# Gated linear attention and a squared-ReLU layer on one core: wider tiles for y of the first eight blocks, and another written-out order

## The chip, the cores and the metric

The kernel runs on one core of a Trainium2 chip. The metric is the device time of one execution in microseconds (us). Three runs of the kernel before gave 184.23, 184.34 and 184.44 us; the median is 184.34 us. Names of engines: PE multiplies matrices (PEld are its weight loads), DVE is VectorE, ACT is ScalarE, POOL is GpSimd, SP issues the DMAs.

## What is computed

The reference has two parts. The first is a recurrence over 768 time steps for 4 batches and 8 heads of 48 channels:

```
state = alpha[t, :, None] * state + outer(k[t], v[t])
y[t]  = q[t] @ state
```

The second takes y of all heads as rows of 384 numbers (3,072 rows) and computes

```
h = x @ w_in                        # 384 -> 2048
g = s * max(h, 0)**2 + b
out = g @ w_out                     # 2048 -> 384
```

All inputs and the output are in float32; the kernel multiplies in bfloat16.

## The kernel before

**Blocks.** The 3,072 rows are cut into 24 blocks of 128 rows, numbered n; six blocks make one batch. Blocks 0 to 7 are worked on as four pairs m = 0 to 3 (functions with a 2 in their name), with even and odd time steps in two halves s and with the two blocks c of the pair in rows 0 to 63 and 64 to 127. Blocks 8 to 23 are worked on one by one (functions with a 1).

**The attention of a block.** `ln2` (ACT) takes logarithms of alpha; `cum2` and `blk2`, or `cumA` (PE), sum them along time; `eb` and `ei` (ACT) turn the sums into factors; `mul` (DVE or POOL) scales q and k with them. For pairs 0 to 2, `T2` transposes q and k on PE and `Tc2` copies the result out of PSUM; pair 3 and the single blocks are transposed by a DMA (`T1`, line 616). `A2` or `A1` (PE, lines 496 and 638) multiply k by q, `mk` (DVE) masks the result into `am`. `KV2` or `KV1` (PE, lines 481 and 625) make the sum over k and v, and `t1` (DVE) and `sn` (POOL or DVE) carry the state on.

**y.** `y2(m)` (line 544) makes y of a pair, and `y1(n)` (line 660) that of a single block. The values v lie in `vp`, which has for each pair p of heads a row of VW = 144 columns: 48 values of one head, 48 zeros, 48 values of the other. y2 makes its output in tiles of 32 channels: a product takes 32 columns of `vp` as weights (64 rows, one block c) and 128 columns of `am`. Sixteen entries of the list `OWN` say which head (p, e) adds to which tile x; with two halves s and two blocks c these are 64 products of 64 rows by 32 columns in each pair. Where a tile of 32 reaches past a head's 48 channels, the zeros of `vp` are in the product. Twelve products with the state follow for each block that has one (line 556, 128 rows by 32 columns). Outputs go to the PSUM banks py (c = 0) and ct (c = 1). `ye` copies y from there to `xd`.

**The second part.** Two blocks make a group g (12 groups). `mm1(g,u,w)` (line 732, six products) makes one of eight units u of h into the bank h_ps[w]; `re` (ACT line 742 or DVE line 744) takes the maximum with zero and `sq` (DVE or POOL line 761, ACT line 759) squares it into `gt`. `mm2(n,jq)` (line 766, four products) adds a quarter of w_out's rows to block n's output in o_ps[n % 2]; `oe` (DVE, line 775) scales and adds the bias, `st` stores. The last block is made in two halves (`mm2h`, `oeh`, `sth`).

**Weights.** `ld_i` and `ld_o` load w_in and w_out in four parts each into staging tiles; `cih` and `co` cast them to bfloat16 (lines 333 and 335); `cp`, `ca` and `cf` (line 359) sum w_out's rows for the bias, and `bmm` and `bc` (lines 379 and 384) spread that sum over o_ps[1] and into `bias_w`.

**Order.** The string PROGRAM holds the whole order, written out by hand: each word calls a function, with its arguments and often the engine behind dots (`re.0.3.0.0.ACT`: group 0, unit 3, bank 0, buffer 0, on ACT). Every engine and SP's DMA queue takes its own words strictly in that order and waits at the first whose inputs are not there. `F.n.w.bank` are fillers: n products of zeros, w columns wide, into a bank that is free. `c_...` words set constants, among them `c_vp` (POOL, line 268), which writes the zeros of `vp`. Below, a word such as mm1.0.6 stands for group 0, unit 6; bank and buffer are left out where they do not matter.

Of the kernel before, what the change touches and what calls it, by code (L numbers as in the profile page):

```python
# [37 lines left out]
mul2.q.1.0.DVE A2.0.0.a c_s.0 mk2.0.1.0 ld_o.1 mul2.k.1.0.POOL mk2.0.1.1 F.2.480.c T2.1.0.o0 mk2.0.0
KV2.0 mul2.k.1.1.POOL Tc2.1.0.o0.ACT ld2.a.2 t1.0 c_t1.1 vc2.1.1.ACT F.2.296.c T2.1.1.o1 vc2.1.0.ACT
y2.0 Tc2.1.1.o1.DVE ld2.v.2 t1.1 A2.1.1.o ye.1.ACT A2.1.0.a ye.0.ACT sn.1.POOL mk2.1.0 cih.1.1.ACT KV2.1  # L40
c_V2 cih.1.0.ACT mm1.0.3.0 t1.2 ld2.q.2 mm1.0.2.1 mk2.1.1.0 sn.2.POOL re.0.3.0.0.ACT mk2.1.1.1
cih.0.0.ACT cih.0.1.POOL t1.3 sq.0.3.0.ACT ld2.k.2 c_ones sn.3.DVE re.0.2.1.1.ACT F.5.456.a0 y2.1
cp.1.DVE ld_o.0 mm1.0.1.0 ye.2.ACT ye.3.DVE ln2.2 mm1.0.0.1 co.1.DVE ld_i.3 sq.0.2.1.ACT cum2.2.1
re.0.1.0.2.DVE cum2.2.0 re.0.0.1.0.ACT blk2.2 ld_i.2 vc2.2.1.DVE eb2.2.1 mm1.1.2.0 sq.0.1.2.DVE ei2.2.0
mm1.1.3.1 sq.0.0.0.DVE ei2.2.1 ld_o.3 mul2.q.2.1.DVE re.1.2.0.1.ACT el2.2 eb2.2.0 mm1.1.0.0
mul2.k.2.1.DVE sq.1.2.1.ACT mul2.k.2.0.DVE re.1.3.1.2.ACT mul2.q.2.0.DVE T2.2.1.y ld2.a.3 vc2.2.0.DVE
T2.2.0.c Tc2.2.1.y.ACT mm1.1.1.1 co.0.POOL Tc2.2.0.c.DVE sq.1.3.2.ACT KV2.2 re.1.1.1.0.DVE A2.2.0.a
re.1.0.0.1.ACT ld_o.2 cp.0.POOL mk2.2.0 mm2.0.0 sq.1.1.0.ACT cih.3.0.ACT mm2.0.1 t1.4 A2.2.1.a
cih.3.1.ACT mm1.0.6.1 sq.1.0.1.DVE ld2.v.3 sn.4.POOL mk2.2.1 mm1.0.7.0 ld_bs re.0.6.1.2.ACT cih.2.1.DVE
mm1.1.7.1 re.0.7.0.0.ACT cih.2.0.DVE sq.0.7.0.ACT mm1.1.6.0 ld2.k.3 ca.0.1.DVE re.1.7.1.1.ACT y2.2  # L50
sq.1.7.1.ACT sq.0.6.2.DVE ld2.q.3 cp.3.DVE re.1.6.0.0.ACT mm1.1.5.1 ye.4.ACT sq.1.6.0.POOL ye.5.DVE
mm1.0.4.0 ln2.3 re.1.5.1.2.DVE re.0.4.0.1.ACT cum2.3.1 co.3.DVE ld1.v.9 mm1.2.3.1 sq.0.4.1.ACT
sq.1.5.2.ACT mm1.0.5.0 co.2.POOL re.2.3.1.0.DVE ld2.a.4 eb2.3.1 cum2.3.0 re.0.5.0.1.DVE ei2.3.1 blk2.3
bsm mm1.2.0.1 sq.2.3.0.ACT bsc vc2.3.0.POOL ld2.a.6 ei2.3.0 mm1.2.5.0 sq.0.5.1.DVE re.2.0.1.2.ACT
cp.2.DVE mm2.0.2 vc2.3.1.ACT ld1.k.9 re.2.5.0.0.ACT mul2.k.3.0.DVE mm1.2.6.1 sq.2.0.2.ACT mul2.k.3.1.DVE
mm1.1.4.0 mul2.q.3.1.DVE eb2.3.0 mm2.0.3 re.2.6.1.1.ACT ca.2.3.DVE T1.7 sq.2.5.0.ACT mm1.2.1.1
mul2.q.3.0.DVE el2.3 re.1.4.0.2.ACT KV2.3 ca.0.2.DVE T1.6 sq.1.4.2.ACT mm1.2.4.0 sq.2.6.1.ACT cf.DVE
re.2.1.1.0.DVE bmm ld1.q.11 ld1.q.10 sq.2.1.0.POOL mm1.2.7.1 bc ld1.k.10 oe.0 mm2.1.0 ld1.k.11
re.2.4.0.2.DVE mm2.1.1 t1.6 sq.2.4.2.ACT mm2.1.2 ln2.4 mm2.2.0 A2.3.0.a mm2.1.3 mk2.3.0 ld1.k.8 mm2.2.1
re.2.7.1.1.DVE mm2.2.2 ld1.v.10 t1.7 A2.3.1.a mm2.2.3 ld1.q.8 mk2.3.1 mm1.2.2.0 ld1.q.9 oe.1 y2.3 blk2.4  # L60
ld1.v.8 ye.6.DVE ye.7.ACT mm2.3.0 re.2.2.0.0.ACT oe.2 cumA.4 ld2.a.5 sq.2.2.0.POOL mm2.3.1 st.0 ei1.9
ei1.8 mm1.3.5.1 mul1.k.9.DVE ld1.v.12 sq.2.7.1.ACT mul1.k.8.DVE mm1.3.7.0 el2.4 re.3.5.1.2.ACT ld1.q.13
sn.7.POOL mm2.3.2 eb1.8 re.3.7.0.0.ACT mul1.q.8.DVE mm1.3.4.1 ln2.6 sq.3.5.2.DVE T1.8 mm2.4.0
re.3.4.1.1.DVE vc1.8.POOL eb1.9 mm2.3.3 vc1.9.POOL st.1 mul1.q.9.DVE KV1.8 mm1.3.6.0 t1.8 T1.9 mm1.3.1.1
re.3.6.0.2.ACT sq.3.4.1.DVE sn.8.POOL KV1.9 ln2.5 mm2.4.1 oe.3 st.2 c_U sq.3.7.0.ACT t1.9 mm1.3.0.0
ld2.a.7 re.3.1.1.1.ACT sq.3.6.2.DVE blk2.5 mm2.5.0 ld1.q.12 sn.9.POOL ld1.q.14 cumA.5 sq.3.1.1.DVE A1.8
vc1.10.POOL eb1.10 mm1.3.3.1 mk1.8 ei1.10 mm2.5.1 ei1.11 re.3.0.0.0.ACT mul1.k.10.DVE mm2.5.2 eb1.11
mul1.q.10.DVE re.3.3.1.2.ACT mm2.5.3 sq.3.0.0.DVE T1.10 sq.3.3.2.ACT mul1.k.11.DVE mm1.3.2.0
mul1.q.11.DVE KV1.10 oe.5 mm2.4.2 re.3.2.0.1.ACT T1.11 t1.10 el2.5 mm2.4.3 ln2.7 sq.3.2.1.POOL A1.9 oe.4
ld1.k.13 mm2.7.0 sn.10.POOL mk1.9 st.4 mm2.6.0 ld1.k.12 mm2.7.1 st.3 Ayy.10 ld2.a.11 ld1.v.13 mm2.6.1  # L70
ye.8.DVE ye.9.ACT vc1.12.POOL mk1.10 mm2.7.2 ld2.a.8 mm1.4.1.1 blk2.6 mm1.4.2.0 re.4.1.1.0.ACT
sq.4.1.0.DVE cumA.6 ld1.v.11 re.4.2.0.2.ACT A1.11 mm1.4.4.1 ei1.12 sq.4.2.2.DVE eb1.12 mul1.k.12.DVE
mm2.7.3 el2.6 re.4.4.1.1.ACT mul1.q.12.DVE mm2.6.2 eb1.13 mk1.11 T1.12 mm1.4.3.0 sq.4.4.1.DVE mm1.4.0.1
re.4.3.0.0.ACT mul1.q.13.DVE ld1.q.15 mm2.6.3 vc1.13.POOL ld1.v.14 re.4.0.1.2.ACT sq.4.3.0.DVE mm1.4.6.0
ei1.13 sq.4.0.2.DVE oe.6 KV1.12 mm1.4.7.1 re.4.6.0.1.ACT mul1.k.13.DVE mm2.8.0 vc1.11.POOL t1.12 T1.13
mm1.4.5.0 sq.4.6.1.DVE oe.7 Ayy.12 re.4.5.0.0.ACT ld1.q.16 ld1.k.14 ld2.a.9 mm2.8.1 ye.10.DVE ye.11.ACT
st.5 re.4.7.1.2.ACT sq.4.5.0.DVE blk2.7 mm1.5.4.0 mk1.12 ld1.k.15 KV1.13 mm1.5.5.1 re.5.4.0.1.ACT
sq.4.7.2.DVE mm2.9.0 t1.13 re.5.5.1.0.ACT mm1.5.6.0 sq.5.4.1.DVE sn.13.POOL ld1.v.15 A1.13
re.5.6.0.2.ACT cumA.7 vc1.14.POOL mk1.13 mm1.5.3.1 ld1.v.16 eb1.14 ei1.14 mm1.5.1.0 re.5.3.1.1.ACT
sq.5.6.2.DVE mul1.q.14.DVE mm2.8.2 el2.7 re.5.1.0.2.ACT mul1.k.14.DVE mm2.8.3 eb1.15 sq.5.3.1.DVE T1.14  # L80
ei1.15 sq.5.1.2.DVE mm1.5.2.1 sq.5.5.0.DVE mm2.9.1 re.5.2.1.1.ACT st.6 mul1.k.15.DVE mm1.5.0.0 oe.8
mm2.9.2 re.5.0.0.2.ACT vc1.15.POOL st.8 mm1.5.7.1 st.7 sq.5.0.2.DVE sq.5.2.1.DVE KV1.14 ld1.q.17
mm2.10.0 re.5.7.1.0.ACT t1.14 ln2.8 mm2.10.1 mul1.q.15.DVE mm2.10.2 sq.5.7.0.DVE T1.15 sn.14.POOL Ayy.14
ld1.k.16 mm2.10.3 ye.13.ACT mk1.14 vc1.16.POOL ld1.k.17 ye.12.ACT ld1.q.22 mm2.9.3 ld1.v.22 oe.10
mm1.6.1.0 blk2.8 KV1.15 re.6.1.0.2.ACT mm1.6.4.1 sq.6.1.2.DVE mm1.6.3.0 t1.15 re.6.4.1.1.ACT A1.15 oe.9
sn.15.POOL cumA.8 ld2.a.10 mm1.6.0.1 eb1.16 ei1.16 mul1.q.16.DVE mm2.11.0 re.6.0.1.0.ACT mul1.k.16.DVE
mm2.11.1 eb1.17 sq.6.4.1.DVE T1.16 ei1.17 sq.6.0.0.DVE mm2.11.2 re.6.3.0.2.ACT mul1.k.17.DVE mm2.11.3
el2.8 mk1.15 st.9 mm1.6.2.1 ld1.k.18 ld1.v.17 oe.11 mm1.6.6.0 re.6.2.1.1.ACT KV1.16 mm2.13.0
sq.6.2.1.DVE re.6.6.0.0.ACT t1.16 mm1.6.5.1 mul1.q.17.DVE mm1.6.7.0 sq.6.3.2.DVE T1.17 sn.16.POOL Ayy.16
re.6.7.0.1.ACT ln2.9 ld1.q.18 mm2.12.0 ye.14.ACT ye.15.DVE ld1.q.19 re.6.5.1.2.ACT sq.6.7.1.DVE ld1.k.19  # L90
mm2.13.1 ln2.10 ld1.v.18 sq.6.5.2.DVE mm1.7.0.0 sq.6.6.0.DVE st.10 mk1.16 mm1.7.4.1 vc1.17.POOL
re.7.0.0.1.ACT mm2.13.2 re.7.4.1.2.ACT blk2.9 sq.7.4.2.DVE mm1.7.6.0 ld1.q.23 A1.17 re.7.6.0.0.ACT
cumA.9 mk1.17 mm2.12.1 ei1.19 ld1.v.19 eb1.19 mm1.7.1.1 el2.9 sq.7.0.1.DVE eb1.18 mm2.13.3 ei1.18
mul1.q.18.DVE re.7.1.1.2.ACT mm1.7.7.0 mul1.k.18.DVE sq.7.1.2.DVE T1.18 mm1.7.2.1 mul1.q.19.DVE
re.7.7.0.1.ACT mul1.k.19.DVE mm2.12.2 re.7.2.1.2.ACT sq.7.7.1.DVE mm1.7.3.0 ld1.q.20 ln2.11 oe.13
vc1.18.POOL ld1.k.20 mm2.12.3 sq.7.2.2.DVE re.7.3.0.1.ACT T1.19 mm2.15.0 oe.12 KV1.18 vc1.19.POOL
mm1.7.5.1 ld1.q.21 sq.7.3.1.DVE mm2.14.0 t1.18 st.13 re.7.5.1.2.ACT ld1.v.20 mm2.14.1 st.12 Ayy.18 st.11
ld1.k.21 mm2.15.1 ye.16.ACT ye.17.DVE sq.7.6.0.DVE KV1.19 mm1.8.5.0 sq.7.5.2.DVE mk1.18 mm1.8.6.1
re.8.5.0.1.ACT blk2.10 mm1.8.7.0 re.8.6.1.0.ACT t1.19 A1.19 sq.8.6.0.DVE re.8.7.0.2.ACT cumA.10
sq.8.5.1.DVE mm1.8.3.1 sn.19.POOL mk1.19 el2.10 ei1.20 eb1.20 mm2.14.2 re.8.3.1.0.ACT mul1.k.20.DVE  # L100
# [761 lines left out]
```

## Time and profile before

| | |
|---|---|
| median of three runs | 184.34 us (184.23 to 184.44) |
| the profiled execution, its own time | 184.03 us |
| its span, first to last instruction | 182.3 us |
| PE busy | 171.9 us, 2,309 products |
| DVE busy | 136.6 us |
| ACT busy | 103.8 us |
| POOL busy | 47.2 us |
| products of zeros (fillers) | 21 |
| moved by DMA | 34.96 MB |

The profile counts an engine as busy from the start of an instruction to its modelled end; products overlap, so distances from start to start say more about PE than busy time. A view called the chain of waits follows the work back from the last instruction; the timeline lists instructions by start; a table by stretches gives each engine's busy time in a stretch of the span. Times inside the execution are counted from its first instruction.

### The profile page before, as it was taken

The numbers are of one execution on the slowest core, as the hardware profiler recorded it, in microseconds if no ns is written. First come the engines' busy times: TensorE is split into PE (matmuls) and PEld (weight loads), VectorE is DVE, ScalarE is ACT, GpSimd is POOL, SyncE is SP. The second block draws the span as 40 slices with busy tenths as digits, with TensorE's granted clock in tenths as the row PEclk, the third lists the DMA queues.
The fourth block names the chain that finished last, engine by engine and source line by source line (L and its number), as shares of the span: only waits on it lengthen the run. The fifth ranks groups of instructions, "written<-read, shape, count | busy, mean of one in ns | idle before, by whom it ended". The sixth has DMA issues, their size and how long they took to land.

```text
span 182.3 us, 5580 instructions
## 1 busy us (share of the span) xinstructions
PE 171.9 (94%) x2309; PEld 122.5 (67%) x2309; DVE 136.6 (75%) x257; ACT 103.8 (57%) x204; POOL 47.2 (26%) x79
## 2 busy tenths in 40 slices
...
GB/s 156 325 355 375 276 338 374 365 271 212 196 217 211 156 158 260 163 234 155 214 238 202 190 223 153 151 214 185 250 58 154 79 96 150 2 5 86 0 133 86
DMA packets 101357, 34.96 MB, mean 192 GB/s; under 512 B 94548, under 2 KB 99796, under 8 KB 101332
## 3 DMA queue, kind: packets, MB, share of 16 engines
...
q8 instruction: 18, 0.29, 0.6%
q14 instruction: 7, 0.06, 0.1%
...
## 4 chain that ended last, share of the span: by engine, by line
PE 75%; DVE 10%; DMA 6%; SPq 3%; issue 3%; POOL 1%; ACT 1%; DVEq 0%; POOLq 0%
PE o_ps L766 31%; PE h_ps L732 28%; SPq L294 3%; DMA qkT<-qk 3%; PE a_ps L638 3%; DMA k_in<-in_k_dram 3%; DVE colsum L359 3%; DVE am L509 2%; PE py_ps L660 2%; PE ct_ps L660 2%; PE ct_ps L571 2%; PE py_ps L625 1%; POOL qk L447 1%; DVE t L701 1%; DVE r L744 1%
## 5 line engine op out<-in xcount | busy, mean ns | idle before, releaser
L732 PE MATMUL h_ps<-xd,w_in_bf 128*128 128x256 bf16 x576 | 74.2, 273 | 0.8 <-DVE r L744 0.6
L742 ACT ACTIVATE r<-h_ps 128x512 bf16<-128x512 f32 x87 | 51.8, 599 | 40.7 <-PE h_ps L732 36.8
L766 PE MATMUL o_ps<-w_out_bf,gt 128*128 128x384 bf16 x368 | 69.3, 326 | 0.1
L732 PEld LDWEIGHTS <-w_in_bf 128*128 128x128 bf16 x576 | 54.6, 98 | 13.7 <-issue 2.9
L766 PEld LDWEIGHTS <-gt 128*128 128x128 bf16 x368 | 34.3, 98 | 19.4 <-issue 0.9
L761 DVE TENSOR_TENSOR gt<-r 128x512 bf16<-128x512 bf16 x74 | 34.3, 484 | 13.4 <-ACT r L742 12.8
L711 POOL TENSOR_TENSOR s_st<-t,blast 128x384 bf16<-128x384 bf16 x15 | 14.6, 971 | 38.8 <-DVE t L701 35.8
L647 DVE TENSOR_TENSOR am<-a_ps,U 128x1024 bf16<-128x1024 f32 x16 | 19.5, 1219 | 3.8 <-PE a_ps L638 3.7
L335 POOL CAST vp<-v_in 128x384 bf16<-128x384 f32 x18 | 11.6, 646 | 33.4 <-DMA v_in<-in_v_dram 24.4
L775 DVE SCALAR_TENSOR_TENSOR o_sb<-o_ps,bs,bias_w 128x384 f32<-128x384 f32 x23 | 14.1, 613 | 3.8 <-PE o_ps L766 2.2
L759 ACT ACTIVATE gt<-r 128x512 bf16<-128x512 bf16 x18 | 11.1, 628 | 3.8 <-DVE r L744 3.7
L333 ACT ACTIVATE xd<-ct_ps 128x384 bf16<-128x384 f32 x6 | 2.9, 490 | 15.2 <-PE ct_ps L660 8.6
L394 ACT ACTIVATE la<-a_in 128x768 bf16<-128x768 f32 x12 | 10.1, 841 | 2.4 <-DMA a_in<-in_alpha_dram 2.4
L761 POOL TENSOR_TENSOR gt<-r 128x512 bf16<-128x512 bf16 x4 | 4.7, 1164 | 23.3 <-ACT r L742 12.3
L595 DVE TENSOR_TENSOR qk<-k_in,binv 128x384 bf16<-128x384 f32 x16 | 9.7, 612 | 1.2 <-ACT binv L585 1.1
L509 DVE TENSOR_TENSOR am<-a_ps,mask 128x1024 bf16<-128x1024 f32 x6 | 7.3, 1223 | 3.9 <-PE a_ps L496 3.7
L595 DVE TENSOR_TENSOR qk<-q_in,b_s 128x384 bf16<-128x384 f32 x16 | 9.7, 606 | 0.6 <-ACT b_s L581 0.4
L701 DVE TENSOR_TENSOR t<-py_ps,s_st 64x192 bf16<-64x192 f32 x26 | 9.2, 353 | 0.9 <-PE py_ps L625 0.5
L335 DVE CAST xd<-ct_ps 128x384 bf16<-128x384 f32 x6 | 3.3, 556 | 5.1 <-PE ct_ps L660 5.0
L447 DVE TENSOR_TENSOR qk<-q_in,b_s 128x384 bf16<-128x384 f32 x7 | 3.8, 556 | 4.3 <-ACT b_s L424 4.3
L824 PE MATMUL a_ps<-zeros 128*128 128x504 bf16 (+3 forms) x17 | 5.7, 478 | 1.3 <-DVE zeros L215 1.3
L333 ACT ACTIVATE xd<-py_ps 128x384 bf16<-128x384 f32 x8 | 3.9, 487 | 5.0 <-PE py_ps L660 3.6
...
## 6 DMA issues: line engine op xcount, KB each, us to landing
...
```

The lines of the kernel that those rows point to most:

```text
L335: {"DVE": nc.vector, "POOL": nc.gpsimd}[eng].tensor_copy(out=out, in_=in_)
L509: nc.vector.tensor_tensor(out=o, in0=i, in1=mask2[s].rearrange("a t p -> a (t p)").unsqueeze(1).to_broadcast([128, n, 128]), op=ALU.mult,)
L595: on(eng).tensor_tensor(out=half_of(qk, n)[:, "qk".index(x), :, 0:D], in0=half_of(ins[x], n).rearrange("a (h d) -> a h d", d=D), in1=half_ ...
L647: nc.vector.tensor_tensor(out=half_of(am, n).rearrange("a e p t -> a (e p) t"), in0=a_ps.rearrange("a e (p t) -> a (e p) t", t=128), in1=U ...
L701: nc.vector.tensor_tensor(out=t1_sb[n % 2][r, :, w], in0=p_ps[r, :, w], in1=s_sb[(n - 1) % 4][r, :, w], op=ALU.add,)
L711: on(eng).tensor_tensor(out=s_sb[n % 4], in0=t1_sb[n % 2], in1=bl.unsqueeze(2).to_broadcast([128, NP, 96]), op=ALU.mult,)
L732: nc.tensor.matmul(out=h_ps[w][:, i * n : (i + 1) * n], lhsT=w_in_bf[:, kk, 128 * j : 128 * (j + 1)], rhs=xd_sb[g % 3][:, kk, 0:n], start= ...
L742: nc.scalar.activation(out=r_sb[i], in_=h_ps[w], func=AF.Relu)
L759: nc.scalar.activation(out=unit_out(g, u), in_=r, func=AF.Square)
L761: on(eng).tensor_tensor(out=unit_out(g, u), in0=r, in1=r, op=ALU.mult)
L766: nc.tensor.matmul(out=o_ps[n % 2][:, 0:d_model], lhsT=gt_of(n)[:, j, c0 : c0 + C], rhs=w_out_bf[:, j, :], start=(j == 0), stop=(j == NJ - 1),
L775: nc.vector.scalar_tensor_tensor(out=out_sb[n % 3], in0=o_ps[n % 2][:, 0:d_model], scalar=s_col, in1=bias_w, op0=ALU.mult, op1=ALU.add,)
```

## The change

The layout `vp` gets 48 more columns of zeros for each pair of heads (VW = 192), so that a window of 64 columns can run past a head at either side. y2 makes y of all four pairs in tiles of 64 channels: twelve entries in `OWN64`, two tiles at a time, which with the two blocks makes four products in a row for four different quarters of the array; with s there are 48 products of 64 by 64 in each pair instead of 64 of 64 by 32. The products with the state and those of the single blocks keep their 32 columns. The order of the words is another one from the first to the last, and some words have another engine: re on DVE 7 instead of 9 (ACT 89 instead of 87), ye on DVE 11 instead of 10, vc2 (the copy of v) on ACT 7, DVE 0, POOL 1 instead of 4, 2, 2, mul2 on POOL 4 instead of 3, cih on POOL 2 instead of 1. The sq keep their numbers (74 on DVE, 18 on ACT, 4 on POOL), though not their places. The fillers are 18 products instead of 21.

```diff
-VW = 144
+
+VW = 192
+Y64 = (0, 1, 2, 3)
...
-c_zeros ld2.a.0 c_act c_qk.1 c_half c_vp.1 ld2.a.1 c_qk.0 ld2.q.0 c_la.1 ld2.k.0 c_la.0 c_s.2 c_t1.0
...
+c_zeros ld2.a.0 c_act c_la.0 c_half c_s.0 ld2.a.1 c_la.1 ld2.q.0 c_qk.0 c_qk.1 ld2.k.0 c_U2 c_ident
+ln2.0 ld2.q.1 c_vp.1 c_t1.0 F.8.504.a0 cum2.0.0 c_vp.0 ld2.k.1 ln2.1 blk2.0 c_mask2 cum2.0.1 eb2.0.0
+cum2.1.0 ld2.v.0 mul2.q.0.0.DVE eb2.0.1 cum2.1.1 ei2.0.0 blk2.1 mul2.q.0.1.DVE el2.0 ei2.0.1 ld_i.1
+mul2.k.0.0.DVE F.1.240.a0 T2.0.0.c eb2.1.1 mul2.k.0.1.DVE eb2.1.0 ei2.1.0 T2.0.1.y ld2.v.1
+mul2.q.1.1.POOL el2.1 Tc2.0.0.c.ACT Tc2.0.1.y.DVE ld_i.0 mul2.k.1.0.POOL ei2.1.1 F.1.504.a0 A2.0.1.o
+A2.0.0.a mk2.0.1.1 mul2.k.1.1.POOL vc2.0.0.ACT ld2.a.2 mk2.0.1.0 vc2.0.1.ACT mul2.q.1.0.POOL mk2.0.0
+F.2.504.c KV2.0 T2.1.1.o1 c_t1.1 t1.0 c_s.2 T2.1.0.o0 ld_o.1 Tc2.1.1.o1.ACT c_V2 Tc2.1.0.o0.DVE y2.0
+cih.1.0.ACT t1.1 ld2.v.2 A2.1.0.a A2.1.1.o ye.1.DVE sn.1.POOL vc2.1.1.ACT mk2.1.1.0 ye.0.ACT c_ones
+mk2.1.1.1 vc2.1.0.ACT cih.1.1.ACT ld2.q.2 F.2.504.h0 KV2.1 mm1.0.2.1 t1.2 cih.0.0.ACT ld2.k.2 mk2.1.0
+sn.2.POOL re.0.2.1.0.ACT F.2.296.o1 mm1.0.0.0 ln2.2 cih.0.1.POOL mm1.0.3.1 t1.3 re.0.0.0.1.ACT
+sq.0.2.0.DVE y2.1 ld_o.0 re.0.3.1.2.ACT sn.3.DVE mm1.0.1.0 cp.1.DVE ye.2.ACT ld_i.3 ye.3.ACT cum2.2.1
...
     def c_vp(i):
-        nc.gpsimd.memset(vp[i][:, :, :, D : 2 * D], 0.0)
+        nc.gpsimd.memset(
+            vp[i].rearrange("a s p (x d) -> a (s p) x d", d=D)[:, :, 1:4:2, :], 0.0
+        )
...
+    OWN64 = [
+        (0, 0, 0), (0, 1, 1), (0, 1, 0), (1, 0, 1), (1, 0, 2), (2, 0, 3),
+        (1, 1, 2), (2, 1, 3), (2, 1, 4), (3, 1, 5), (3, 0, 4), (3, 0, 5),
+    ]
...
+        v2 = whole(vp, m).rearrange("a s p f -> a s (p f)")
         states = [c for c in range(2) if (2 * m + c) % NCH]
-
-        for i0 in range(0, 16, 4):
+        own, w = (OWN64, 64) if m in Y64 else (OWN, 32)
+        g = 128 // w
+
+        for i0 in range(0, len(own), g):
             for s in range(2):
-                for i in range(i0, i0 + 4):
-                    p, e, x = OWN[i]
-                    c0 = 32 * x - 96 * p + 48 * e
+                for i in range(i0, i0 + g):
+                    p, e, x = own[i]
+                    c0 = VW * p + w * x - 96 * p + 48 * e
                     for c in range(2):
                         r = slice(64 * c, 64 * c + 64)
                         nc.tensor.matmul(
-                            out=y_out(y_ps(c), x),
-                            lhsT=v2[r, s, p, c0 : c0 + 32],
+                            out=y_out(y_ps(c), x, w),
+                            lhsT=v2[r, s, c0 : c0 + w],
                             rhs=a2[r, s, e, p, :],
```

Where the steps of the prediction need later parts of the two orders, these are they. Loads of the kernel before, in their order: a.0 a.1 q.0 k.0 q.1 v.0 k.1 v.1 w_in 1, 0, w_out 1, a.2 v.2 q.2 k.2, w_out 0, w_in 3, 2, w_out 3, a.3, w_out 2, v.3. Of the changed one: a.0 a.1 q.0 k.0 q.1 k.1 v.0, w_in 1, v.1, w_in 0, a.2, w_out 1, v.2 q.2 k.2, w_out 0, w_in 3, 2, w_out 3, a.3, w_out 2, and later v.3. DVE's words in the kernel before, after `mk2.2.0`: t1.4 sq mk2.2.1 cih.2.1 cih.2.0 ca.0.1 sq cp.3 ye.5 re.1.5 co.3 re.2.3 re.0.5 bsc sq cp.2, two mul2.k, mul2.q, ca.2.3, mul2.q, ca.0.2, cf. In the changed one: t1.4 sq ca.0.1 mk2.2.1 cih.2.1 cp.3 ye.4 re.1.5 co.3 sq cp.2 re.0.5 re.2.0 bsc, mul2.k, mul2.q, sq, mul2.q, mul2.k, ca.2.3 ca.0.2 cf t1.6 bc.

178 lines of the change are left out of this document (85 added, 93 removed).

## The prediction

> **What bounds the kernel now.** I read the page's busy shares first, then the table by stretches of 10 us, then the chain of waits, then timelines around its odd steps.
>
> ```profile
> PE 171.9 (94%) x2309; PEld 122.5 (67%) x2309; DVE 136.6 (75%) x257; ACT 103.8 (57%) x204; POOL 47.2 (26%) x79
> ...
> q8 instruction: 18, 0.29, 0.6%
> ```
> ```profile
> 10.00:20.00 10.00, 7.16 (x207) 5.32 (x208) 7.17 (x14) 5.89 (x11) 5.89 (x13) 1.00 1.09 363
> 20.00:30.00 10.00, 8.99 (x180) 6.61 (x177) 9.43 (x19) 8.55 (x18) 4.61 (x6) 1.00 1.01 322
> 30.00:40.00 10.00, 9.66 (x185) 7.13 (x173) 9.83 (x14) 9.24 (x17) 5.93 (x5) 1.00 1.10 343
> 40.00:50.00 10.00, 9.30 (x85) 6.61 (x81) 9.52 (x18) 6.29 (x15) 1.53 (x2) 1.00 0.88 200
> 50.00:60.00 10.00, 10.00 (x172) 6.28 (x171) 7.25 (x11) 4.24 (x10) 2.19 (x3) 1.00 0.97 209
> ```
>
> The columns are PE, PEld, DVE, ACT, POOL, granted clock, DMA share, GB/s. From 50 us on PE has no idle time but 0.22 us near 86. Up to 50 us it lacks 2.15, 2.84, 1.01, 0.34 and 0.70 us: first DMA, then DVE (9.4 to 9.8 of 10) sets the pace. So the end is where PE stands at about 48 us plus a fixed amount of work, and an order can win only ahead of 50 us. The chain says where:
>
> ```profile
> 15.39 2.09 issue
> 17.48 0.31 PE a_ps L496 x5
> ...
> 46.30 0.57 DVE colsum L359
> 46.92 0.93 PE o_ps L379 x2
> ...
> 48.54 2.76 PE o_ps L766 x16
> ...
> 80.69 5.27 DMA qkT<-qk
> ```
>
> The 2.09 us stand in the middle of A2.1.0, after 223 products, where no semaphore is waited for. Queue q8 moves 18 blocks of 16 KB, or 64 bytes for each of PE's 4,618 loads and products; its first block starts at 15.28 in the trace. I read it as PE having no instructions. At 46.3 cf (DVE) releases bmm and, by bc, mm2.1.0 at 48.54. Before both lies a gate that no order moves:
>
> ```profile
> 26.98 2.58 POOL L335 CAST w_out_bf<-gt 128x1536 bf16<-128x1536 f32 x1 [5.39 <-DMA gt<-in_moe_w_out_dram]
> 29.52 1.81 POOL L359 TENSOR_TENSOR colsum<-gt 128x768 f32<-128x768 f32 x1
> ```
> ```profile
> 29.72 0.42 PE L496 MATMUL a_ps<-qkT 64*64 64x128 bf16 x16
> 30.07 1.47 PE L766 MATMUL o_ps<-w_out_bf,gt 128*128 128x384 bf16 x8
> ```
>
> co.0 and cp.0 run as soon as w_out's part 0 lands; mm2.0.0 needs co.0 (29.56) and ca.0.1 needs cp.0 (31.33). The same bytes are ahead of that load in both orders.
>
> **y in wider tiles.**
>
> ```profile
> 34.80 0.23 PE L544 MATMUL py_ps<-am,vp 64*32 64x128 bf16 x1
> 34.80 0.23 PE L544 MATMUL ct_ps<-am,vp 64*32 64x128 bf16 x1
> ...
> 35.46 0.35 PE L556 MATMUL py_ps<-qkT,s_st 128*32 128x128 bf16 x12
> ```
>
> Today 64 products take 0.66 us up to the state's: 32 start in four lots of eight at 34.80, .86, .92 and .97, the others singly, 8 ns apart. A2 has the new shape, 64 by 64 with 128 columns: 16 products in four lots of four, 0.25 us from A2 to A2 (14.81 to 15.06), 0.35 us up to a product of another shape. Lots of four follow as slowly as lots of eight, 0.056 to 0.06 us, so twelve cost 0.35 + 8 x 0.056 = 0.80 us at most and 0.08 + 11 x 0.056 + 0.08 = 0.78 at least by these rows. I take +0.12 us for each pair. From the other side, 48 products at the 8 ns of the second half would be 0.55 us, -0.11. Only y2.2 and y2.3 lie where PE sets the pace.
>
> The zeros: memsets of 128, 256 and 384 columns take 0.20, 0.31 and 0.42 us, so 768 take about 0.74, +0.64 us for two, hidden in POOL's idle 5.71 to 9.18. Uncovered, they would delay mul2.q.1.1 by as much.
>
> **The order up to 30 us.** k.1 is issued one place (1.19 us) earlier and lands near 10.2 instead of 11.4, v.0 the other way. POOL then runs q.1.1 (9.18), k.1.0, k.1.1 and the added q.1.0, 1.0 us each, to 13.15 instead of 13.48; T2.1 behind it ends at 13.65. DVE's t1.1 follows Tc2 as before (14.66). KV2.0 waits for vc2.0, now both on ACT behind v.0: 12.4 instead of 11.96. A2.1 can run near 14.8, and mk2.1 need not wait until 17.82. KV2.1 waits on ACT: Tc2.1.1 to 14.4, cih.1.0 to 15.2, then vc2.1.1, ye.0, vc2.1.0 to 16.45. There PE's first stock ends: 223 products now fall three short of KV2.1's end (16.5) and no longer into A2.1. When the next block is usable is the unknown. Before, it was usable (17.48) 5.9 us after product 88; product 88 is now in KV2.0, at 12.2. That gives 18.15. The second block came 5.75 us after the same place of its stock, instead of 3.74, which gives 20.15; if the smaller loads now ahead let it through sooner, 16.5. I take 18.15, the first block's own delay. Then t1.2, mk2.1.0, t1.3 (0.71, 1.23, 0.71) free y2.1 at 21.1 (before: 21.69), with one more mm1 already done and the filler of 1.13 us gone. mul2.k.2 waits for k.2 (near 25.0); T2.2, Tc2.2, A2.2.0 end at about 28.4, KV2.2 at 28.9, and mm2.0.0 starts at co.0's 29.6 instead of 30.07: **-0.47 us**. Some 0.1 to 0.7 us of slack is left. Fillers lie in waits and cost nothing.
>
> **From 30 to 48 us.** ca.0.1 is moved ahead of mk2.2.1 and waits for cp.0 (31.33); behind it on DVE stand mk2.2.1 (now to 33.4), cih.2.1, cp.3, ye.4. Only y2.2 waits for mk2.2.1, and PE gets there at 34.2 (34.80 before, and the four mm1 ahead keep their spacing by re on ACT), so the wait is covered by 0.8 us. DVE's work from 31.33 to cf's end shrinks from 15.5 us by t1.4 and a sq (done sooner), cih.2.0, re.2.3 and two sq, and grows by re.2.0 and two other sq: 13.6 us plus about 1.1 us of waits for y2.2 and re.1.5's product, cf's end at 46.05 instead of 46.86. ACT took over what DVE lost, near 2.5 us where it had 0.8 + 3.7 idle; its late vc2.3 and re.1.4 hold KV2.3 and mm1.2.1 until 45.75, so bmm starts at 46.4 (46.92 before), bc ends at 47.95, mm2.1.0 starts at 48.0: **-0.54 us in all** at this point, y2.2 counted.
>
> **From 48 us to the end.** mm2.1.0 to the last product took 130.17 us. Summed over start-to-start distances by kinds of neighbours, the old order gives 129.92 and the new one 129.81 plus y2.3's 0.12. The 0.26 that are left were Ayy.12's wait for its transpose, behind four loads issued in the 3.3 us before it; the new order has one load in that time, so I let it go. T1 to A1 is otherwise 4.7 to 8 us of PE's work in both orders. Ending and last store are as before.
>
> **Sum.** -0.54 + 0.12 - 0.11 - 0.26 = -0.79, against the profiled execution: span 182.3 plus 1.7 around it, 184.03, gives 183.2. The runs' median is 0.31 above that execution: **183.5 us**.
>
> **Rivals.**
> 1. *PE's instructions come late (slower).* The last three products of KV2.1 hold t1.2, and by it mk2.1.0 and y2.1. With 20.15 y2.1 starts at 23.1, and the 0.1 to 0.7 us of slack is overrun by some 1.6: mm2.0.0 at 31.2, 1.1 us later than before. DVE's shorter list regains 0.3: 185.1. It decides from a block usable after 18.9. For it: three of the first blocks came 3.7, 5.75 and 4.4 us late; against: the loads just ahead are small. 0.2. [...]
> 2. *The transposes are late.* T1.8, T1.12 and T1.14 have 5.1, 4.74 and 4.73 us until their A1 (5.6, 4.75, 5.4 before). If each took T1.12's 5.27, PE would wait 0.2 + 0.5 + 0.5 in place of 0.26: 184.4, no change. 0.16.
> 3. *More is won.* If ACT does not hold KV2.3, bmm starts at cf's 46.05 and mm2.1.0 at 47.65; with y at -0.11 instead of +0.12 twice: 182.7. DVE's list speaks for it, ACT's 9.24 of 10 against. 0.13.
> 4. *PE slows down.* Fillers fall from 9,544 to 8,344 columns. After the 2.3 us gap PE's mm1 still took 0.66 us, so the idle of before did no harm; the first fillers, of 504 columns, start 0.42 us apart, those near 9.5, of 480, 0.2 us, so PE has a slower state. In it up to 22 us PE would lose some 1.5 us, half of it hidden: 185. 0.03. [...]
>
> The forecast keeps 0.48, from 183.0 to 183.95. About 0.2% (0.37 us) is what a measurement of this kernel can tell from no change. Faster: 0.45 of the forecast's and rival 3's 0.13, 0.58; same: 0.03 of the forecast's and 0.14 of rival 2's, 0.17; slower: rivals 1 and 4 and 0.02 of rival 2's, 0.25. The range from 182.5 to 185.1 takes in rival 3's y and rival 1's late block.
>
> **What would show it.** y2.2 from first product to first state product at 0.78; no idle in A2.1.0 but one at KV2.1's end, gone by 18.2; mm2.0.0 at 29.6; cf's end at 46.05 and bmm at 46.4; mm2.1.0 at 48.0; no PE idle near 86. I am wrong if KV2.1 ends after 19, if mm2.0.0 starts after 30.1, or if PE idles behind 50 us.

## The result, and the profile after

The changed kernel is slower. Twenty runs have a median of 185.79 us (184.29 to 191.03), against 184.74 us (183.49 to 188.20) for twenty runs of the kernel before beside them. The ratio is 1.0055, with a 95% interval of 1.0034 to 1.0076: some 1.0 us lost, where 0.8 us of gain was forecast. Executions far above the others of their kernel are left out of this and every later ratio; the four profiled executions of the changed kernel happened to be long ones (187.46 to 189.15 us), so its parts are also read below in two kernels that share one half of its order each.

One of the four, of 188.84 us (the kernel is called e15 below). First lines of its page:

```profile
PE 173.5 (93%) x2242; PEld 123.3 (66%) x2242; DVE 133.8 (71%) x252; ACT 105.7 (56%) x208; POOL 46.8 (25%) x80
...
PEclk9999699999999999999999999999999999999999
...
q8 instruction: 17, 0.28, 0.6%
```

The table by stretches has the columns of the table before:

```profile
10.00:20.00 10.00, 6.78 (x184) 4.84 (x185) 7.31 (x15) 5.97 (x12) 6.26 (x15) 0.98 1.09 365
20.00:30.00 10.00, 9.87 (x146) 7.29 (x145) 9.14 (x14) 8.10 (x17) 4.39 (x5) 0.85 0.98 305
30.00:40.00 10.00, 8.96 (x163) 6.70 (x164) 9.67 (x14) 8.86 (x16) 7.11 (x5) 1.00 1.09 346
40.00:50.00 10.00, 9.48 (x92) 7.05 (x90) 9.51 (x18) 8.04 (x18) 0.13 (x1) 1.00 0.94 207
...
80.00:100.00 20.00, 19.32 (x235) 14.47 (x230) 16.35 (x35) 12.79 (x27) 1.47 (x2) 1.00 1.11 208
100.00:125.00 25.00, 22.62 (x298) 15.99 (x297) 16.77 (x31) 11.70 (x24) 5.08 (x7) 1.00 0.96 189
```

What PE waited for, first from 10 to 50 us, then from 50 us on (us in total, number of times, the longest):

```profile
PE ct_ps L486 <- issue: 1.7, 1, 1.7
...
PE a_ps L501 <- ACT gt L773: 0.9, 1, 0.9
```
```profile
PE a_ps L652 <- DMA qkT<-qk: 2.9, 4, 1.2
```

Three things are new. The pause in which PE waits for nothing that the profile shows is still there (1.7 us), now in KV2.1 (line 486), and a stretch of 3.41 us at half clock (granted: 0.50) follows it from 19.55. A2.2.0 (line 501) waits 0.9 us just ahead of mm2.0.0; the view names ACT's sq (done at 30.85), but DVE's copy Tc2.2.0.c, which A2.2.0 reads, ended only 0.06 us earlier. And behind 50 us, where PE had 0.22 us of idle time, it waits four times for a transpose, 2.9 us in all.

A good measure for the second part is the time from mm2.1.0's start to the end of PE's last product. It is 130.67 us in the kernel before and 134.24 us here; mm2.1.0 itself starts at 49.76 instead of 48.54. In the other three profiled executions of the changed kernel the second part took 131.5, 131.9 and 134.3 us, with mm2.1.0 at 51.18, 52.44 and 49.37 (the last, e4, with a stretch at half clock from 103.57, right behind a wait of 1.8 us for a transpose): an early start of the second part was paid back in it. Without PE's waits in it the second part takes 130.45 us in the kernel before, 131.17 us in e15 (0.15 us at Ayy.12, which the view leaves out, taken off too), and 130.5 to 131.2 us in every other profile below but one (e4, with that stretch at half clock in it). So what differs behind mm2.1.0 from kernel to kernel is mostly what PE waits for.

Where the first part goes wrong is seen on DVE and POOL. DVE's timeline of e15, then POOL's (start, duration):

```profile
27.56 0.56 DVE L452 TENSOR_TENSOR qk<-k_in,binv 128x384 bf16<-128x384 f32 x1 [0.43 <-ACT binv L432]
28.03 0.55 DVE L452 TENSOR_TENSOR qk<-q_in,b_s 128x384 bf16<-128x384 f32 x1
28.50 1.68 DVE L775 TENSOR_TENSOR gt<-r 128x512 bf16<-128x512 bf16 x1
30.11 0.68 DVE L340 COPY qkT<-ct_ps 128x1024 bf16<-128x1024 bf16 x1
```
```profile
28.19 1.72 POOL L340 CAST w_out_bf<-gt 128x1536 bf16<-128x1536 f32 x1 [4.29 <-DMA gt<-in_moe_w_out_dram]
29.88 1.98 POOL L364 TENSOR_TENSOR colsum<-gt 128x768 f32<-128x768 f32 x1
```

sq.1.2.2 (line 775) takes 1.68 us instead of the 0.42 or 0.43 of others, and ends at 30.18, 0.27 us behind POOL's co.0 (28.19 to 29.91). Behind it Tc2.2.0.c (line 340) has its input since 29.31 and starts at 30.11.

### The profile page after: what moved, and what is told of

The parts are those of the page before. It is cut to its first block, busy times and chain, and to the rows that moved or that the text cites. A ratio compares the mean times of both kernels' runs of the same rounds, so it can differ in the third digit from the quotient of the medians.

```text
span 187.4 us, 5445 instructions
## 1 busy us (share of the span) xinstructions
PE 174.6 (93%) x2242; PEld 124.1 (66%) x2242; DVE 135.3 (72%) x252; ACT 105.7 (56%) x208; POOL 46.8 (25%) x80
## 4 chain that ended last, share of the span: by engine, by line
PE 80%; DMA 8%; DVE 3%; SPq 3%; ACT 3%; issue 2%; ACTq 0%; DVEq 0%
PE h_ps L746 32%; PE o_ps L780 31%; DMA qkT<-qk 5%; SPq L299 3%; PE a_ps L652 3%; DMA v_in<-in_v_dram 3%; PE py_ps L674 2%; PE ct_ps L585 2%; PE ct_ps L674 1%; DVE qk L452 1%; PE py_ps L558 1%; PE py_ps L639 1%; DVE gt L775 1%; PE ct_ps L420 1%; PE a_ps L501 1%
## 5 line engine op out<-in xcount | busy, mean ns | idle before, releaser
L756 ACT ACTIVATE r<-h_ps 128x512 bf16<-128x512 f32 x89 | 52.6, 598 | 46.5 <-PE h_ps L746 36.5
L746 PE MATMUL h_ps<-xd,w_in_bf 128*128 128x256 bf16 x576 | 75.4, 276 | 0.4 <-DVE r L758 0.2
L780 PE MATMUL o_ps<-w_out_bf,gt 128*128 128x384 bf16 x368 | 70.9, 330 | 0.1
L746 PEld LDWEIGHTS <-w_in_bf 128*128 128x128 bf16 x576 | 55.2, 99 | 13.1 <-issue 1.4
L725 POOL TENSOR_TENSOR s_st<-t,blast 128x384 bf16<-128x384 bf16 x15 | 14.0, 930 | 64.7 <-DVE t L715 54.3
L340 POOL CAST vp<-v_in 128x384 bf16<-128x384 f32 x17 | 9.7, 586 | 23.1 <-DMA v_in<-in_v_dram 13.7
L775 POOL TENSOR_TENSOR gt<-r 128x512 bf16<-128x512 bf16 x4 | 4.1, 1039 | 14.9 <-ACT r L756 14.9
L652 PEld LDWEIGHTS <-qkT 64*128 64x128 bf16 x128 | 4.0, 94 | 5.0 <-issue 2.4
L652 PE MATMUL a_ps<-qkT 64*128 64x128 bf16 x128 | 6.3, 218 | 1.0 <-DMA qkT<-qk 1.0
L340 DVE CAST xd<-py_ps 128x384 bf16<-128x384 f32 x5 | 2.8, 558 | 5.7 <-PE py_ps L674 4.0
```

The lines of the kernel that those rows point to most:

```text
L340: {"DVE": nc.vector, "POOL": nc.gpsimd}[eng].tensor_copy(out=out, in_=in_)
L652: nc.tensor.matmul(out=a_ps[:, e, 128 * p : 128 * p + 128], lhsT=T[r, 1, p, :], rhs=T[r, 0, p, :], start=True, stop=True,)
L725: on(eng).tensor_tensor(out=s_sb[n % 4], in0=t1_sb[n % 2], in1=bl.unsqueeze(2).to_broadcast([128, NP, 96]), op=ALU.mult,)
L746: nc.tensor.matmul(out=h_ps[w][:, i * n : (i + 1) * n], lhsT=w_in_bf[:, kk, 128 * j : 128 * (j + 1)], rhs=xd_sb[g % 3][:, kk, 0:n], start= ...
L756: nc.scalar.activation(out=r_sb[i], in_=h_ps[w], func=AF.Relu)
L775: on(eng).tensor_tensor(out=unit_out(g, u), in0=r, in1=r, op=ALU.mult)
```

## The experiments

Each kernel was compared with the kernel before on the same chip, those with neighbouring numbers together (e1 to e3, e4 to e7, e8 to e11, e12 to e15, e16 to e18). "The old order" and "the new order" are the two PROGRAM strings.

### Tiles and order apart: e1, e2, e3

e1 is the changed kernel. e2 takes back the order, e3 the tiles:

```diff
 PROGRAM = the old order                  # e2
-Y64 = (0, 1, 2, 3)                       # e3
+Y64 = ()
```

> The changed kernel itself, for an undisturbed profile beside the other two. Order theory (the loss lies in the order: KV2.1's last products come late, then the sums for mm2.0.0, then transposes behind 50 us): about 1.0 us slower than before, mm2.0.0 after 30.1, mm2.1.0 after 48.6, PE idle at two A1 behind 90 us, 1.6 us of it. Tile theory (the loss is y's tiles): mm2.0.0 as before or earlier, no more PE idle than before behind 50 us, and 0.25 us more in each of y2.0 to y2.3. Clock theory (fewer products of zeros let the clock halve): a stretch of 3.4 us with the clock granted at 0.5 ahead of 36 us in this profile too.

> The order of the kernel before, with y2 in 64-column tiles and the wider vp. Tile theory: 0.8 to 1.0 us slower than before. Order theory: y2.2 and y2.3 cost 0.12 us each, 0.25 us slower at most; with 16 products fewer in y2.0 PE's first stock of instructions (223 products) ends behind A2.1.0, in or ahead of KV2.1, so the 2.09 us pause moves there, and from 0.5 us of gain to 0.3 us of loss can come of that.

> The changed order, with y2 in 32-column tiles as before (64 products in each pair; vp keeps the 48 more zero columns). Tile theory: as before or up to 0.3 us faster than before. Order theory: 0.7 to 1.2 us slower than before; with 16 products more ahead of KV2.1 the first stock ends ahead of KV2.1's first product or in its first ones instead of in its middle, and the pause stands there, as long as in the changed kernel within 1 us.

**e2, the tiles alone, is faster than the kernel before: 0.9953 (0.9920 to 0.9986), some 0.9 us.** e3, the order alone, is far slower: 1.0293 (1.0245 to 1.0341), 5.4 us. e1, the changed kernel itself, has six executions (184.06 to 191.71 us) and no ratio; its profile has PE's wait of 0.66 us at Ayy.14. So the tile theory falls, and the order is what costs. My numbers were off all the same: I allowed e2 at most 0.5 us of gain and e3 at most 1.2 us of loss.

y2's own price is as predicted: y2.2 and y2.3 are 0.13 and 0.14 us longer from their start to PE's next word. What e2 gains fits the 16 products that y2.0 no longer issues ahead of PE's pause. PE's waits in e2 ahead of 50 us:

```profile
PE ct_ps L485 <- issue: 1.1, 1, 1.1
```

The pause is 1.1 us instead of 2.1 and lies in KV2.1; t1.2 starts at 18.16 instead of 18.96, mm2.0.0 at 29.27 instead of 30.07, mm2.1.0 at 47.41 instead of 48.54. Four later kernels with the tiles, the old order up to there and no stretch at half clock start mm2.1.0 at 47.48 to 47.74 (e8, e10, e13, e17). In e3 the same arithmetic works against the kernel: product 223 falls into A2.1.1, the pause there is 3.2 us, KV2.1 starts at 19.68, two mul2 meet co.0 and cp.0 (1.32 and 2.15 us instead of 0.55), and mm2.1.0 starts at 52.55.

### Three edits of the new order: e4 to e7

e4 is the changed kernel again. e5 lets DVE's four mul2 run in a row ahead of co.0 and gives the sq to ACT, e6 has four fillers fewer ahead of KV2.1, e7 issues one load later:

```diff
-... ei2.2.0 ... re.1.2.1.2.ACT ... ei2.2.1 ... eb2.2.0 ... sq.1.2.2.DVE T2.2.0.c    # e5
+... ei2.2.0 ei2.2.1 eb2.2.0 ... re.1.2.1.2.ACT ... T2.2.0.c ... sq.1.3.0.ACT sq.1.2.2.ACT
-F.8.504.a0                                                                        # e6
+F.4.504.a0
-ld1.k.17 ... T1.14                                                                # e7
+T1.14 ld1.k.17
```

> The changed kernel again, so that the next three stand beside it on one chip, and for a profile without a halved clock ahead of 50 us. Lock theory (POOL's co.0 and cp.0 hold DVE's mul2.q.2.0 and sq.1.2.2 back, because the changed order leaves a gap in DVE's row of mul2): where mul2.q.2.0 starts behind co.0 it takes 1.8 us instead of 0.55 and sq.1.2.2 takes 2.0 instead of 0.42, and mm2.0.0 starts 2 to 3 us later than before's 30.07; where it starts ahead of co.0, only the sq is held. Clock theory: the loss is there only where a stretch at half clock lies ahead of 36 us, and without one the kernel is as fast as before.

> The changed kernel with ACT's ei2.2.1 and eb2.2.0 ahead of re.1.2.1, so that DVE's four mul2 run in a row ahead of co.0, and with sq.1.2.2 on ACT behind sq.1.3.0 instead of on DVE ahead of Tc2.2.0.c. Lock theory: no DVE instruction between 25 and 32 us takes over 0.75 us but mk2; mm2.0.0 starts 1.5 to 2.5 us earlier than in the changed kernel, and the time falls by 1.0 to 2.5 us. Clock theory and fetch theory: the stall of 1.2 to 1.6 us at A2.2.0 has other causes, so 0.3 us at most either way.

> The changed kernel with four products of zeros fewer ahead of KV2.1 (F.4.504.a0 for F.8.504.a0): product 223 then lies behind KV2.1's end instead of three products ahead of it. Fetch theory: KV2.1 ends near 17.4 instead of 18.8, t1.2 and t1.3 come 1.0 to 1.4 us earlier, the pause stands behind KV2.1, and the time falls by 0.5 to 1.5 us. Lock theory: what is gained at KV2.1 counts only where it brings mul2.q.2.0 ahead of co.0; else 0.3 us at most. If the pause is no matter of the number of products, it stays inside KV2.1.

> The changed kernel with the load ld1.k.17 issued behind the transpose T1.14 instead of just ahead of it. Transpose theory: PE's wait of 0.66 us at Ayy.14 goes, and the time falls by 0.4 to 0.7 us. If PE's later words wait for something else anyway, no change.

The ratios are 1.0032 (0.9987 to 1.0076) for e4, 1.0092 (1.0059 to 1.0125) for e5, 1.0152 (1.0103 to 1.0201) for e6 and 1.0019 (0.9972 to 1.0066) for e7. **Two edits did at their place what they should, and no time came of it.** In e5 no DVE instruction in this row takes longer than usual any more:

```profile
26.04 1.02 DVE L452 TENSOR_TENSOR qk<-k_in,binv 128x384 bf16<-128x384 f32 x2
26.98 0.55 DVE L452 TENSOR_TENSOR qk<-q_in,b_s 128x384 bf16<-128x384 f32 x1
28.51 0.69 DVE L340 COPY qkT<-ct_ps 128x1024 bf16<-128x1024 bf16 x1 [0.97 <-PE ct_ps L464]
```

mm2.0.0 starts at 30.05 and mm2.1.0 at 48.62. In e6 product 223 lies behind KV2.1, as counted: KV2.1 ends at 17.36 and mm2.0.0 starts at 29.10; by mm2.1.0 (48.61) nothing of that is left. But behind 50 us PE then waits for transposes for 2.7 us in e5 and for 3.1 us in e6:

```profile
PE a_ps L652 <- DMA qkT<-qk: 3.1, 4, 1.1
```

The second part takes 133.9 and 134.3 us. By their ratios both are slower still than the changed kernel, e5 within the intervals, e6 beyond them; why, these runs do not settle. e7 shows nothing: T1.14 is issued 0.87 us behind its mul1 (0.85 in e1), and Ayy.14 still waits 0.59 us. One load was not the cause.

### Half of the order each: e8 to e11

All with the 64-column tiles. e8 has the old order up to A1.11 (near 78 us) and the new one behind it, e9 the reverse; the few words that only one half holds stand at the seam. e10 is e8 with four loads behind T1.14, e11 is e2 with two loads behind T1.12:

```diff
-ld1.k.16 ... ld1.q.17 ... ld1.q.16 ... ld1.k.17 ... T1.14      # e10
+T1.14 ld1.k.16 ld1.q.17 ld1.q.16 ld1.k.17
-ld1.v.13 ... ld2.a.8 ... ld1.v.11 ... T1.12                    # e11
+ld1.v.11 ... T1.12 ld2.a.8 ld1.v.13
```

> y in 64-column tiles; the order of the kernel before up to A1.11 (near 78 us), the changed order from there. Theory of two losses (ahead of 50 us PE's sums come late in the changed order; behind 80 us its transposes are issued behind more loads, and PE waits for them the longer, the earlier it arrives): 1.5 to 3.5 us slower than the old order with 64-column tiles, nearly all of it as PE's waits for DMA transposes between 85 and 130 us. Theory that all is lost ahead of 50 us: as the old order with 64-column tiles within 0.7 us.

> y in 64-column tiles; the changed order up to A1.11, the order of the kernel before from there. Theory of two losses: mm2.1.0 as in the changed kernel (48.6 to 52), PE's wait for transposes behind 80 us at most 0.6 us, and the time 0.5 to 2.5 us below that of the changed kernel where its first part is alike, 0.5 to 3 us above that of the old order with 64-column tiles. Theory that all is lost ahead of 50 us: as the changed kernel within 0.7 us.

> As the kernel of the old order up to A1.11 and the changed one behind it, but with the four loads k.16, q.17, q.16 and k.17 issued behind the transpose T1.14 instead of between T1.13 and T1.14. If the loads ahead of a transpose make it late: T1.14 is issued when mul1 is done, Ayy.14 waits under 0.2 us, and the time falls by 0.7 to 1.5 us unless T1.15 or T1.16 is late in its place. If the transposes are late by the total of bytes moved by then: the wait moves to Ayy.16 or A1.17 in full and the time stays.

> The old order with 64-column tiles, and the loads a.8 and v.13 issued behind the transpose T1.12 instead of ahead of it. If loads ahead of it make a transpose late: PE's 0.57 us at Ayy.12 goes, and the time is 0.3 to 0.6 us below that of the old order with 64-column tiles, 1.1 to 1.5 us below the kernel before. If Ayy.12 then waits for v.11 or T1.13 is late in its place: no change.

**The loss is in the half behind 78 us.** e8 gives 1.0057 (1.0022 to 1.0092), as the whole change; e9 gives 0.9965 (0.9930 to 1.0000), near e2 (in its profile Ayy.12 waits 0.89 us for T1.12, more than the 0.6 us expected). By quotients, the new second half costs 1.0057 / 0.9953, some 1.9 us, behind the old first half, and 1.0055 / 0.9965, some 1.7 us, behind the new one. The new first half costs 0.9965 / 0.9953, some 0.2 us, less than the intervals can tell, and not the 0.5 us or more that was expected (by single profiles mm2.1.0 starts at 48.98 in e9 and at 47.41 in e2, so this stays open). In e8's profile PE waits twice (its timeline):

```profile
86.20 0.40 PE L652 MATMUL a_ps<-qkT 64*128 64x128 bf16 x8 [1.34 <-DMA qkT<-qk]
...
101.19 0.40 PE L652 MATMUL a_ps<-qkT 64*128 64x128 bf16 x8 [1.20 <-DMA qkT<-qk]
```

That is 2.54 of the 2.7 us by which its second part (133.35 us) is longer than that of the kernel before. Not all of it is the new order's, though. The first row below, the load a.9, stands at e8's seam, right ahead of T1.12, where neither order has it, and in the four profiles of the changed kernel Ayy.12 waits 0, 0, 0 and 0.15 us. So much of the 1.34 us belongs to the seam, and the 1.9 us are too high by it. In e9 a store at the seam (st.4, 81.11) stands in the same way ahead of T1.12, whose late issue (1.45 us) is seen in the wait of 0.89 us; that can only make the 1.7 us too low. SP's queue in e8 shows how they come about (start, time that SP was busy with the issue):

```profile
80.32 1.02 SPq L299 DMA_DIRECT2D a_in<-in_alpha_dram  x1
81.46 1.84 SPq L630 DMA_TRANSPOSE qkT<-qk  x1
83.34 0.57 SPq L288 DMA_DIRECT2D q_in<-in_q_dram  x1
83.95 1.64 SPq L829 DMA_DIRECT2D out_dram<-o_sb  x2
85.70 1.30 SPq L630 DMA_TRANSPOSE qkT<-qk  x1
87.05 2.97 SPq L288 DMA_DIRECT2D k_in<-in_k_dram  x3
```

There is no gap over 0.12 us: SP issues without a stop, 18.9 of the 20 us from 80 to 100 (18.2 in the kernel before). T1.12 (81.46) is issued 1.5 us behind the end of its mul1, T1.13 (85.70) 3.0 us; before, these were 0.25 and 0.97 us. The new order has st.5 (83.95) ahead of T1.13, and by T1.14 it has issued k.16, q.17 and k.17, where the old one has only v.16 (74 words against 72). T1.13's delay costs PE nothing here; T1.14's does, though it is issued only 0.38 us behind its mul1:

```profile
94.82 1.68 SPq L630 DMA_TRANSPOSE qkT<-qk  x1
96.54 2.22 SPq L829 DMA_DIRECT2D out_dram<-o_sb  x2
```

It lands 6.3 us after its issue, and Ayy.14 starts at once. In the four profiles of the changed kernel T1.14 is issued 0.85 to 1.44 us late and lands 5.0 to 5.9 us after that, and Ayy.14 waits 0.66 to 1.81 us. So two things add up: the issue is late, and the transfer takes long (in e9 T1.14 lands 2.75 us after its issue).

e10 moved the wait instead of removing it: T1.14 is issued 0.06 us behind its mul1 and Ayy.14 does not wait, but T1.15 to T1.17 are 1.7 to 3.3 us late, and PE waits at Ayy.16 (0.61) and A1.17 (1.45). Its ratio is 1.0090 (1.0047 to 1.0133). Ayy.12, ahead of the moved loads, waited 2.14 us, where e8 with the same words up to there has 1.34: single executions differ by most of a microsecond at this place. e11 (0.9964, 0.9927 to 1.0000) is no gain over e2: T1.12 is in time (0.08 us), but the load v.13 that I had moved holds vc1.13 on POOL, vc1.11 stands behind that, and Ayy.12 waits 1.4 us for vc1.11.

### Stores off SP's queue, and the sq beside co.0 in the old kernel: e12 to e18

e12, e13, e14 and e15 ran together. e12 (new order) and e13 (old order with the tiles) issue the stores of blocks 0 to 10 from ACT. e14 is the kernel before with one sq moved to DVE, e15 the changed kernel again:

```diff
-                nc.sync.dma_start(                          # e12, e13: ACT; e16, e17: nc.gpsimd
+                (nc.scalar if n <= 10 else nc.sync).dma_start(
-... vc2.2.0.DVE T2.2.0.c Tc2.2.1.y.ACT ... Tc2.2.0.c.DVE sq.1.3.2.ACT       # e14
+... vc2.2.0.DVE sq.1.3.2.DVE T2.2.0.c Tc2.2.1.y.ACT ... Tc2.2.0.c.DVE
```

> The changed kernel with the stores of blocks 0 to 10 issued from ACT's queue instead of SP's. If SP's queue makes the transposes late: SP is busy at most 16 of 20 us between 80 and 100, the transposes T1.12 to T1.17 are issued within 0.5 us of their mul1, PE waits for them under 0.4 us in all behind 80 us, and the time is 0.7 to 2.5 us below the changed kernel's, unless ACT is then late with re (PE waits for ACT instead, 0.5 us or more). If bandwidth is short: the waits of 0.7 to 3 us stay.

> The old order with 64-column tiles, with the stores of blocks 0 to 10 issued from ACT's queue. If SP's queue makes the transposes late: PE's 0.67 us of waits behind 50 us go, and the time is 0.3 to 0.7 us below that of the old order with 64-column tiles, 1.1 to 1.6 us below the kernel before. If bandwidth is short, or ACT becomes late: as the old order with 64-column tiles, or up to 0.7 us slower.

> The kernel before with one edit: sq.1.3.2 is done by DVE ahead of Tc2.2.0.c instead of by ACT, so that an instruction with two inputs in SBUF meets POOL's co.0 and cp.0. Lock theory: sq.1.3.2 takes 1.3 to 3 us instead of 0.42, Tc2.2.0.c and mm2.0.0 come 0.8 to 2 us later, and the time rises by 0.3 to 1.5 us (ACT has 0.6 us less work). If there is no lock: sq.1.3.2 takes 0.42 us, Tc2.2.0.c starts at T2.2.0's end as before, and the time stays within 0.3 us.

> The changed kernel once more, for a profile without a halved clock ahead of 50 us. Theory of two losses: mm2.1.0 between 48.6 and 49.5, sq.1.2.2 held to 1.5 us or more, and 1.0 to 3 us of PE's waits for DMA transposes between 85 and 125 us. If the first part is what loses: mm2.1.0 above 50 and under 0.7 us of such waits.

In e12 PE waits for no transpose behind 50 us, with the same loads and stores, so the amount of bytes alone is not what made them late. But the time stays, 1.0061 (1.0021 to 1.0101). The exception that was named is there: an issue of two DMAs holds ACT for 1.1 to 2.0 us (e12 and e13; in e13 one lasts from 86.70 to 88.73, and ACT's next instruction starts at 88.78), and PE waits once for ACT, right behind such issues. It also waits once for DVE; that these two waits are all that holds the time is not shown.

```profile
PE h_ps L746 <- ACT r L756: 0.5, 1, 0.5
PE py_ps L558 <- DVE am L514: 0.5, 1, 0.5
```

e13 (0.9958, 0.9921 to 0.9994) is like e2; PE waits 1.0 us for ACT at mm1.5.5 in it. e15's two executions, 188.84 and 188.96 us, are too few to compare; its profile was shown above. The two losses are both in it, though the mm2.1.0 of 49.76 is a little past the stretch expected.

**The sq beside co.0 costs time in the old order too.** e14 is 1.0078 (1.0036 to 1.0120), 1.4 us slower, by one sq. Its DVE, then its POOL:

```profile
28.55 1.53 DVE L761 TENSOR_TENSOR gt<-r 128x512 bf16<-128x512 bf16 x1
30.01 0.68 DVE L335 COPY qkT<-ct_ps 128x1024 bf16<-128x1024 bf16 x1
```
```profile
28.25 1.55 POOL L335 CAST w_out_bf<-gt 128x1536 bf16<-128x1536 f32 x1 [6.67 <-DMA gt<-in_moe_w_out_dram]
```

The sq starts 0.30 us behind co.0 and ends 0.28 us behind it, after 1.53 us; Tc2.2.0.c comes at 30.01 instead of 28.68, mm2.0.0 at 31.09 instead of 30.07, mm2.1.0 at 49.56 instead of 48.54. (A stretch at half clock from 17.94 in e14 had made DVE's row of mul2 end 0.25 us later, so about that much of the delay is not the sq's; and the second part lost 0.7 us at two transposes.) The instructions on DVE whose input is in PSUM, Tc2 (0.68) and mk2 (1.22), keep their time beside POOL's cp.0 (29.77 to 31.75).

e16 (new order) and e17 (old order with the tiles) issue those stores from POOL; e18 is e2 with only the stores of blocks 3, 4 and 5 on ACT, in pauses of ACT.

> The changed kernel with the stores of blocks 0 to 10 issued from POOL's queue. If SP's queue is the cause of the loss and POOL has room: SP busy under 16 of 20 us between 80 and 100, no wait for a transpose over 0.3 us behind 80 us, no wait for ACT either, and the time 0.8 to 2 us below the changed kernel's, at or below that of the kernel before. If something else in the changed order's second half costs time too: the waits go and the time stays, as in e12. POOL late with sn or vc1 would show as PE waiting for them at KV1 or y.

> The old order with 64-column tiles, with the stores of blocks 0 to 10 issued from POOL's queue. If SP's queue is the cause of its 0.67 us of waits: they go, and the time is 0.3 to 0.8 us below that of the old order with 64-column tiles, 1.1 to 1.7 us below the kernel before. If POOL is held up: PE waits for sn or vc1, no gain or a loss up to 1 us.

> The old order with 64-column tiles, with only the stores of blocks 3, 4 and 5 issued from ACT's queue, in pauses of ACT (st.5 five words earlier). If SP's queue is the cause: T1.12 and T1.13 are issued within 0.3 us of their mul1, no PE wait behind 50 us over 0.2 us, and the time is 0.3 to 0.7 us below that of the old order with 64-column tiles, 1.1 to 1.6 us below the kernel before. If not: as the old order with 64-column tiles.

e16's SP, where e8's was shown:

```profile
81.71 1.29 SPq L630 DMA_TRANSPOSE qkT<-qk  x1
83.06 0.57 SPq L288 DMA_DIRECT2D q_in<-in_q_dram  x1
84.63 1.24 SPq L630 DMA_TRANSPOSE qkT<-qk  x1
85.92 2.03 SPq L288 DMA_DIRECT2D k_in<-in_k_dram  x3
```

SP is busy for 13.2 of 20 us, each of T1.12 to T1.18 is issued within 0.08 us of its mul1 and takes SP 1.23 to 1.29 us, and those whose landing the trace holds land 2.8 to 4.0 us after their issue. PE waits for nothing behind 50 us, and **the second part takes 131.00 us, against 131.5 to 134.3 in the four profiles of the changed kernel, which differs only in the engine of these stores.** The time is 1.0017 (0.9984 to 1.0050). That is some 0.7 us below the changed kernel's, a little less than expected, and with intervals that overlap it is not clear of noise; nor is it at or below the kernel before. e16's first part still starts mm2.1.0 late (49.52, with a stretch at half clock behind the pause). e17 is 0.9977 (0.9936 to 1.0017), e18 is 0.9958 (0.9922 to 0.9995). Their second parts take 130.69 and 130.52 us, shorter than e2's 131.33, but e2, e13, e17 and e18 cannot be told apart by their ratios; the 0.3 to 0.8 us below e2 that e17 and e18 were to show are not seen. Any of e2, e13 and e18 is faster than both kernels: about 0.4% below the one before, about 1% below the changed one.

## Why the prediction was wrong

Single executions differ by 1 us (the profiled one of the kernel before was 184.03 us, runs of it beside these kernels have means of 184.9 to 185.5 us). So places are compared below by profiles, gains by ratios.

- **The step that failed: "the new order has one load in that time, so I let it go. T1 to A1 is otherwise 4.7 to 8 us of PE's work in both orders."** It made the stretch behind 48 us shorter by 0.25 us and put the transposes at nothing; by the changed kernel and e9 the new second half costs 1.7 us (0.8 us either way). At Ayy.12 itself the forecast held. What failed was to take 4.7 to 8 us as enough everywhere else: from the end of its mul1 to its landing T1.14 took 6.2 to 7.3 us in the four profiles, and PE waited at Ayy.14 in all of them, and at A1.13, Ayy.16 and A1.17 in some, 0.7 to 3.1 us in all. I had looked at the loads right ahead of one transpose, and not at what stands in SP's queue at each of them: a transpose is issued late there (0.85 to 1.44 us for T1.14), and it lands late. With the same order and the stores off SP's queue (e16) the waits are gone. That takes work from SP and transfers from the same DMA queue (2.16 MB, which e16 has in q0 instead of q1) at once, so which of the two matters more stays open. This was rival 2's mechanism. I gave it 0.16 and "184.4, no change", but the forecast of 183.5 had already taken the 0.26 off, so its own waits of 1.2 us make 184.7, slower than before.
- **"A gate that no order moves."** Wrong, and this made the second error. co.0's 2.58 us were not fixed: it takes 1.47 us in e5, where it starts as DVE's row of mul2 ends (27.53), and 2.58 us in the kernel before, where it starts at 26.98 inside that row (to 27.97). In the new order sq.1.2.2, put ahead of Tc2.2.0.c, meets co.0 (1.68 us in e15, 1.69 us in e9). In e15 a mul2 had waited 0.43 us for ei2.2.1, so that the row ended late; in e9 the row has no gap, and the sq meets co.0 all the same. mm2.0.0 was forecast at 29.6; it starts at 30.86 in e9 and at 30.05 in e5, where no sq meets co.0. I priced every moved DVE word at its own duration.
- **30 to 48 us, "-0.54".** cf was to end at 46.05 and mm2.1.0 to start at 48.0. Without half clock they came at 47.31 and 48.98 (e9), 46.94 and 48.62 (e5). ca.0.1, moved ahead as I read it, runs beside POOL's sn.4 and cih.2.0 and takes 1.58 us instead of 0.94.
- **The pause.** The count of 223 products held in every order: the next one came 2.30 us later in the kernel before (15.18 to 17.48, in A2.1.0) and 1.94 us later in the profile of 189.15 us (16.83 to 18.77, three short of KV2.1's end); the pause stood in A2.1.1 with 16 products more (e3, 3.2 us) and behind KV2.1 with four fewer (e6, 1.2 us). That PE had no instructions there stays a reading: the view says "issue". I took 18.15 for the next block; in the kernels with the new first half the product behind the 223 started at 18.50 to 18.79, late, but short of the 18.9 from which rival 1 decides. With full clock t1.3 freed y2.1 at 21.55 to 21.83 (e5, e12, e9), not at the forecast 21.1 and no earlier than before (21.69). So part of rival 1 was there, and the 0.47 us to be won up to 30 us did not come, even with the sq out of co.0's way (e5, 30.05). (The rival's 185.1 leaves out the 0.25 us that the forecast takes off behind 48 us; by its own terms it is 184.9.) The same count fits what the tiles win in e2, which I did not see as a gain of the tiles.
- **y in tiles.** +0.12 us forecast, 0.13 and 0.14 us measured. Right. "More is won" by y at -0.11 did not happen.
- **PE slows down.** A stretch of half clock comes with the pause in all four profiles of the changed kernel (it begins at 18.24 to 19.55), and there moves y2.1 to 22.5 to 22.9. But by their mean clocks 22 of its 39 executions had a stretch at half clock somewhere, and 92 of 134 of the kernel before, so nothing here points at the fillers.

What stays open: why e6 is slower than the changed kernel itself (and e5, if it is); whether e16, with no wait behind 50 us, is truly 1.0 us slower than e9 (1.0017 against 0.9965, 0.9 us either way); and what the new first half costs by itself.
